# Nine on-chip transposes moved from the DMA crossbar to TensorE, and three weight loads cut into fourteen

## Chip, cores, metric

One core of a Trainium2 chip runs the whole program. The metric is the device time of one execution in microseconds (us). Times are medians of several runs; every run carries the granted TensorE clock of its core. A single profiled execution supplies each trace, and its span is about 2 us shorter than its device time.

## The reference

Attention over four batches of eight heads (sequence 768, head width 64), in which each query keeps only six key chunks of 32, followed by a gated MLP with a spatial mixing matrix.

```python
# q, k, v: (4, 8, 768, 64) float32
ub  = sum(maximum(q * k_min_of_chunk, q * k_max_of_chunk))     # bound of each chunk
sel = the 6 chunks with the highest ub, causal
attn = softmax(where(sel & causal, q @ k.T / 8, -1e9))
x = (attn @ v) as (4, 768, 512)
h = relu(x @ w_in); u, v = halves of h
out = (u * (w_spatial @ layernorm(v) + b)) @ w_out
```

## The kernel before

Two heads are one *pair*; there are 16 pairs, four to a batch. The program is written as steps placed on numbered *beats*, twelve beats to a pair, and the build turns them into one fixed instruction order for each engine. An engine works through its order in turn, so an instruction that waits holds up those behind it; one trace below shows PE standing 11.3 us before a single matmul.

The k of every pair but the first, and the attention output x of every pair but the last, are transposed by DMA through the crossbar:

```python
def k_transpose(self):
    src = self.k.rearrange("p h t d -> p (h t d)")
    if self.i == 0:
        kT = ps_ml.tile([P, 2, NQT // 2, P], F16, tag="mlp", name="kTp")     # PSUM
        ...
        for t in range(NQT):
            nc.tensor.transpose(out[:, t * P:(t + 1) * P], src[:, t * P:(t + 1) * P], identity)
    else:
        kT = sb.tile([P, 2, NQT // 2, P], F16, tag="kT", name="kT")           # SBUF
        nc.sync.dma_start_transpose(out=kT.rearrange("d h m s -> d (h m) s"), in_=src)
# ... k_max, k_min, k_operand read kT on VectorE ...
def x_transpose(self):
    ...
    if self.i < NPAIR - 1:
        nc.sync.dma_start_transpose(out=dst.rearrange("p (t s) -> p t s", s=P),
                                    in_=self.x16.rearrange("p t h d -> p (t h d)"))
    else:
        tr = self.trans_tile()
        for t in range(NQT):
            nc.tensor.transpose(tr[:, t * P:(t + 1) * P], self.x16[:, t, :, :], identity)
        nc.vector.tensor_copy(dst, tr)
```

q, k and v come by GpSimd-issued DMA with a cast to 16 bits, two pairs (384 KB after the cast) at a time, each row in pieces of 64 elements. The three weights come whole, between them:

```python
at(1 * BEATS, load_w_in)        # 1024 KB
at(2 * BEATS, load_w_spatial)   # 1152 KB
at(3 * BEATS, load_w_out)       #  512 KB
# ... the first MLP starts at beat 57; its first matmuls read x of pairs 0 to 3 and w_in
```

The softmax here doesn't subtract the row's maximum and nothing guards it: scores larger than these inputs give would overflow.

## Time and profile before

| | before |
|---|---|
| median of the runs | 250.38 us (247.63 to 255.23) |
| the profiled execution | 258.75 us, span 257.0 us, mean clock 0.934, marked slow |
| first MLP matmul | 81.8 us, then a stall until 89.6 us |

The page of the profile cuts the span into 40 slices of 6.4 us; a digit is the busy share in tenths, PEclk the granted TensorE clock in tenths, DMA the busy share of the core's 16 DMA engines ("the rings" below), GB/s what they moved.

```profile
PE   1256677044986399969997789799999999999994
DVE  4995966061679689999999999977556824338530
PEclk9999795755899979988999999999999999999999
DMA  9999999999999999999519520301250010160006
GB/s 60 114 148 145 113 171 126 95 80 101 156 157 126 137 147 126 98 95 140 78 55 182 165 61 4 64 0 33 106 172 18 18 32 3 34 242 2 0 10 237
```

The DMA row is full up to 122 us, while PE and VectorE (DVE) have a hole in the eighth slice. Here the full row stands over a hole: the engines idle while the loads are still under way. The view by windows puts numbers on it. Its columns are length, busy us (and instruction count) of each engine, granted clock, DMA share and GB/s:

```profile
20.00:40.00 20.00, 12.70 (x168) 9.12 (x168) 14.65 (x55) 13.29 (x26) 7.82 (x9) 0.88 2.01 146
40.00:60.00 20.00, 8.19 (x69) 5.63 (x68) 8.31 (x36) 6.02 (x11) 1.56 (x2) 0.59 2.10 90
60.00:80.00 20.00, 15.77 (x207) 12.11 (x208) 12.10 (x49) 13.46 (x28) 5.23 (x5) 0.85 2.31 150
```

From 40 to 60 us no compute engine is busy half the time, and the rings move 90 GB/s against about 150 on either side. The view of waits over the first 100 us names what stood in front of the engines (total us, times, longest):

```profile
DVE qs_84 L160 <- DMA q<-in_q_dram: 10.4, 1, 10.4
DVE kmm L179 <- DMA kT<-k: 5.0, 2, 2.5
PE wtr L341 <- DMA ws_raw<-in_moe_w_spatial_dram: 4.1, 1, 4.1
PE mlp L375 <- DMA xT<-x_960: 3.1, 1, 3.1
```

The DMA view gives KB of one issue and the median us from issue to landing:

```profile
k<-in_k_dram POOLq DMA_DIRECT2D x7, 384.0 KB, 14.6
ws_raw<-in_moe_w_spatial_dram POOLq DMA_DIRECT2D x1, 1152.0 KB, 42.1
w_out_sb<-in_moe_w_out_dram POOLq DMA_DIRECT2D x1, 512.0 KB, 46.5
kT<-k SPq DMA_TRANSPOSE x15, 6.3
```

In this trace a crossbar transpose lands 2.5 to 2.8 us after its issue once the rings are quiet (from 124 us); in the first 90 us it took 6.2 to 23.1 us.

### The profile page before, as it was taken

What the parts mean: (1) busy time and instruction counts of PE and PEld (TensorE: products, weight loads), DVE (VectorE), ACT (ScalarE), POOL (GpSimd) and SP (SyncE); (2) the same over time, 40 slices, a digit from 0 to 9 for tenths busy, and PEclk for the clock granted to TensorE, in tenths of its full rate; (3) what the DMA queues carried; (4) which work ended last, traced back from release to release, by engine and by line L of the source; (5) the groups of instructions that cost most, each with busy time, mean ns of one, the idle gap of its engine ahead of it and who ended that gap; (6) DMA issues with size and microseconds to landing.
All of it is one profiled execution on the core that took longest, in us unless ns stands there. A gap on an engine that the chain in (4) does not pass through costs nothing.

```text
span 257.0 us, 5354 instructions
## 1 busy us (share of the span) xinstructions
PE 203.3 (79%) x2016; PEld 130.1 (51%) x2016; DVE 180.7 (70%) x608; ACT 165.8 (64%) x323; POOL 69.6 (27%) x94
## 2 busy tenths in 40 slices
PE   1256677044986399969997789799999999999994
PEld 0134455034753256636654456567555666645551
DVE  4995966061679689999999999977556824338530
ACT  3947484041796259935687689666899986657213
POOL 8983342022115623153113103111121122200000
PEclk9999795755899979988999999999999999999999
DMA  9999999999999999999519520301250010160006
GB/s 60 114 148 145 113 171 126 95 80 101 156 157 126 137 147 126 98 95 140 78 55 182 165 61 4 64 0 33 106 172 18 18 32 3 34 242 2 0 10 237
DMA packets 103486, 24.74 MB, mean 96 GB/s; under 512 B 98594, under 2 KB 99874, under 8 KB 103460
## 3 DMA queue, kind: packets, MB, share of 16 engines
q0 software_dynamic: 76000, 12.19, 88.4%
q1 hardware_dynamic: 27460, 12.20, 29.5%
q8 instruction: 16, 0.26, 0.5%
q14 instruction: 10, 0.08, 0.1%
HBM read 24.39 MB, written 6.29 MB: 119 GB/s over the span
## 4 chain that ended last, share of the span: by engine, by line
PE 39%; DMA 30%; DVE 20%; POOL 4%; issue 3%; ACT 3%; SPq 0%; POOLq 0%; ACTq 0%
PE mlp L375 27%; DMA q<-in_q_dram 16%; DMA kT<-k 7%; PE sc L263 5%; PE acc L285 4%; DMA k<-in_k_dram 3%; DMA xT<-x_960 3%; DVE kmm L183 2%; DVE kmm L179 2%; DVE stats L387 2%; PE tr L250 2%; ACT e L268 1%; DVE vn L399 1%; DVE rq L214 1%; DVE gT L415 1%
## 5 line engine op out<-in xcount | busy, mean ns | idle before, releaser
L268 ACT ACTIVATE e<-sc 128x512 f16<-128x512 f32 x192 | 99.4, 555 | 35.5 <-PE sc L263 28.6
L275 POOL TENSOR_SCALAR_AFFINE_SELECT e<-e 128x384 f16<-128x384 f16 x48 | 25.6, 535 | 100.5 <-ACT e L268 100.5
L375 PE MATMUL mlp<-wsT,vn 128*128 128x512 f16 (+1 forms) x192 | 42.9, 330 | 0.0
L285 PEld LDWEIGHTS <-e 128*128 128x128 f16 x672 | 33.5, 101 | 17.1 <-POOL e L275 2.3
L375 PE MATMUL mlp<-w_in_sb,xT 128*128 128x512 f16 x96 | 27.3, 400 | 6.7 <-DMA xT<-x_960 3.1
L415 DVE TENSOR_TENSOR gT<-mlp,uT 128x512 f16<-128x512 f32 (+1 forms) x32 | 17.7, 555 | 12.7 <-PE mlp L375 11.9
L375 PE MATMUL mlp<-xT,w_in_sb 128*128 128x512 f16 (+1 forms) x128 | 25.8, 326 | 0.0
L375 PE MATMUL mlp<-w_out_sb,gT 128*128 128x512 f16 x96 | 25.6, 379 | 0.0
L423 ACT COPY o<-mlp 128x512 f32<-128x512 f32 x24 | 14.2, 592 | 14.7 <-PE mlp L375 13.6
L375 PEld LDWEIGHTS <-vn 128*128 128x128 f16 x192 | 18.3, 99 | 10.0 <-DVE vn L399 0.2
L385 ACT ACTIVATE vraw<-mlp 128x512 f32<-128x512 f32 x24 | 14.5, 605 | 11.4 <-PE mlp L375 11.0
L387 DVE BATCH_NORM_STATS2 stats<-vraw 128x6 f32<-128x512 f32 x24 | 16.5, 688 | 7.3 <-ACT vraw L385 7.2
L179 DVE TENSOR_REDUCE kmm<-kT 128x24 f16<-128x768 f16 x15 | 14.2, 945 | 5.0 <-DMA kT<-k 5.0
L375 PEld LDWEIGHTS <-xT 128*128 128x128 f16 x96 | 9.3, 102 | 15.9 <-DMA xT<-x_960 3.4
L315 POOL DMA_DIRECT2D q<-in_q_dram x9 | 12.0, 1337 | 18.5 <-issue 7.4
L315 POOL DMA_DIRECT2D k<-in_k_dram x9 | 12.1, 1348 | 17.3 <-issue 11.9
L407 ACT ACTIVATE uT<-mlp 128x512 f16<-128x512 f32 (+1 forms) x32 | 15.8, 506 | 1.4 <-PE mlp L375 1.4
L375 PEld LDWEIGHTS <-w_in_sb 128*128 128x128 f16 x128 | 11.8, 98 | 6.7
L183 DVE TENSOR_REDUCE kmm<-kT 128x24 f16<-128x768 f16 x15 | 14.1, 942 | 0.0
L285 PE MATMUL acc<-vt_80,e 128*128 128x65 f16 x210 | 12.3, 199 | 2.3 <-POOL e L275 2.1
L399 DVE TENSOR_SCALAR vn<-vraw,mv,rstd 128x512 f16<-128x512 f32 x24 | 12.1, 555 | 0.7 <-ACT rstd L397 0.7
L375 PEld LDWEIGHTS <-gT 128*128 128x128 f16 x96 | 8.6, 98 | 7.1 <-DVE gT L415 0.4
(243 smaller groups left out, 404.4 us busy)
## 6 DMA issues: line engine op xcount, KB each, us to landing
out_dram<-o SPq DMA_DIRECT2D x24, 256.0 KB, 2.1
k<-in_k_dram POOLq DMA_DIRECT2D x7, 384.0 KB, 14.6
q<-in_q_dram POOLq DMA_DIRECT2D x7, 384.0 KB, 13.1
ws_raw<-in_moe_w_spatial_dram POOLq DMA_DIRECT2D x1, 1152.0 KB, 42.1
w_in_sb<-in_moe_w_in_dram POOLq DMA_DIRECT2D x1, 1024.0 KB, 25.4
vt_82<-in_v_dram POOLq DMA_DIRECT2D x2, 384.0 KB, 14.5
vt_83<-in_v_dram POOLq DMA_DIRECT2D x2, 384.0 KB, 27.8
vt_80<-in_v_dram POOLq DMA_DIRECT2D x2, 384.0 KB, 18.3
```

Source lines behind the costliest of these rows:

```text
L179: nc.vector.tensor_reduce(self.kmm[:, 0, :], self.kT.rearrange("d h m (c ch) -> d (h m c) ch", ch=CHUNK), axis=AX.X, op=Alu.max)
L183: nc.vector.tensor_reduce(self.kmm[:, 1, :], self.kT.rearrange("d h m (c ch) -> d (h m c) ch", ch=CHUNK), axis=AX.X, op=Alu.min, negate=True)
L268: nc.scalar.activation(out=self.e[hi][:, g * 512:g * 512 + width], in_=sc[:, 0:width], func=Act.Exp, scale=scale)
L275: nc.gpsimd.affine_select(out=blk, in_=blk, compare_op=Alu.is_ge, fill=0.0, base=0, channel_multiplier=-1, pattern=[[0, 3], [1, P]])
L285: mm(self.av[:, qi, :], lhsT=self.e[hi][:, c:c + P], rhs=self.v[:, hi, t, 0:D + 1], start=(t == 0), stop=(t == qi))
L315: nc.gpsimd.dma_start(out=t[:, 0:n, :, 0:D], in_=src)
L375: mm(st[group][:, 0:cols], lhsT=lhsT, rhs=rhs, start=(j == 0), stop=(j == n - 1))
L385: nc.scalar.activation(st["vraw"][:, ti, :], h, func=Act.Relu)
L387: nc.vector.bn_stats(stats, st["vraw"][:, ti, :])
L399: nc.vector.tensor_scalar(st["vn"][:, ti, :], in0=st["vraw"][:, ti, :], scalar1=st["mv"][:, ti, 0:1], scalar2=st["rstd"][:, ti, :], op0=Al ...
L407: nc.scalar.activation(st["uT"][:, db, t0:t1], h[:, 0:t1 - t0], func=Act.Relu)
L415: nc.vector.tensor_tensor(st["gT"][:, db, t0:t1], in0=vs[:, 0:t1 - t0], in1=st["uT"][:, db, t0:t1], op=Alu.mult)
```

## The change

The intent is to take transposes off the rings while they are full of loads, and to let k, q and v pass between the pieces of the weights.

```diff
-            if self.i == 0:                      # k_transpose
+            if self.i < 6:
-            if self.i < NPAIR - 1:               # x_transpose
+            if 4 <= self.i < NPAIR - 1:
-    def load_w_in():
-        nc.gpsimd.dma_start(out=w_in_sb, in_=moe_w_in.rearrange("(o p) f -> p o f", p=P))
+    def load_w_in(j):
+        nc.gpsimd.dma_start(out=w_in_sb[:, j], in_=moe_w_in[j * P:(j + 1) * P, :])
 ... load_w_spatial(j) and load_w_out(j) likewise ...
-    at(1 * BEATS, load_w_in)
-    at(2 * BEATS, load_w_spatial)
-    at(3 * BEATS, load_w_out)
+    for j in range(NDO):
+        at(12 + 8 * j, load_w_in, j)
+    for j in range(NQT):
+        at(36 + 4 * j, load_w_spatial, j)
+    for j in range(KO):
+        at(62 + 6 * j, load_w_out, j)
     for so in range(NQT):
-        at(4 * BEATS + 2 * so, prep_w_spatial, so)
+        at(5 * BEATS + 2 * so, prep_w_spatial, so)
```

More of the change, by code (lines that the diff above doesn't have):

```diff
@@ L327, with load_w_spatial, load_w_out @@
     brow_l = cp.tile([P, P], F16)
-    def load_w_in():
-        nc.gpsimd.dma_start(out=w_in_sb, in_=moe_w_in.rearrange("(o p) f -> p o f", p=P))
-    def load_w_spatial():
-        nc.gpsimd.dma_start(out=ws_raw, in_=moe_w_spatial.rearrange("(to ti) s -> ti to s", ti=P))
-    def load_w_out():
-        nc.gpsimd.dma_start(out=w_out_sb, in_=moe_w_out.rearrange("(ko ki) f -> ki ko f", ki=P))
+    def load_w_in(j):
+        nc.gpsimd.dma_start(out=w_in_sb[:, j], in_=moe_w_in[j * P:(j + 1) * P, :])
+    def load_w_spatial(j):
+        nc.gpsimd.dma_start(out=ws_raw[:, j], in_=moe_w_spatial[j * P:(j + 1) * P, :])
+    def load_w_out(j):
+        nc.gpsimd.dma_start(out=w_out_sb[:, j], in_=moe_w_out[j * P:(j + 1) * P, :])
     def prep_w_spatial(so):
```

## The prediction

> **What bounds the kernel now.** The span has two stages. From about 90 us on TensorE bounds it: in the ten-us windows PE is busy 155 of the last 167 us. Before 90 us the DMA rings do. The page's DMA row is 9 in every slice up to 122 us, and over 30 to 60 us PE is busy only 15.1 us of 30, VectorE 15.7, ScalarE 13.0; from 46 to 52 us nothing computes. The chain of waits gives DMA 30%, the largest piece being 41.5 us of one q load (issued 35.6, landed 77.1). The list of waits names VectorE for the third group's q, 10.4 us (to 53.4), PE for the spatial weight, 4.1 us (to 61.2), PE for the last x transpose of batch 0, 3.1 us (to 89.6). Idling also leaves PE at a granted clock of 0.5 in most windows from 40 to 66 us; the Trainium skill ("TensorE: Matmul & The Clock Gate", the HAM clock gate) says the clock halves after an idle window, and this trace agrees.
>
> Loads queue behind each other: the spatial weight (1152 KB) takes 42 us from issue to landing, the output weight 46, k and q loads between them 36 to 45. And crossbar transposes slow everything: one takes 2.5 to 2.8 us when the rings are quiet (from 124 us), 6 to 23 us in the first 90. With up to three in flight (44 to 60 us) the rings move 55 to 107 GB/s, against about 150 at 12 to 28 us with zero to two. From the bytes landed (2.9 MB from 26 to 61 us, 20 us at 150 GB/s, in 35 us with four transposes; 2.3 MB from 77 to 98 us, 15 us, in 21 with two and a half) I estimate 2 to 4 us of ring time per transpose. The skill's "DMA: Bandwidth & Descriptors" (Issuing engines are not separate DMA queues) says why: all queues run on the same 16 engines.
>
> **The change.** It removes nine of 29 transposes, all in the DMA-bound stage: an estimated 18 to 36 us of ring time, nearly all critical. Split weights let k, q and v pass between pieces of 128 to 256 KB. It adds: on PE nine times six transposes, about 0.35 us a set warm, 0.8 cold, 4 us in all; on VectorE four x copies from PSUM (0.56 us each) and 20 operand copies 0.1 us dearer, 4 us; on GpSimd eleven more issues of 0.8 us, mostly in idle time. PE now blocks in order on a late k load, and each k tile holds one of three PSUM buffers for 16 beats; both look affordable.
>
> **Sum.** At 145 GB/s the 6.8 MB needed before the first MLP take about 50 us, so VectorE then sets the pace, 9 to 10 us a pair: the first MLP matmul, now at 81.8 with a stall to 89.6, comes at about 65 us. The PE-bound stage behind it stays 163 to 170 us; the transpose waits near 103 to 113 us (6 us) mostly vanish. Gain about 21 us: **229 us**, range 219 to 239. Faster by over 2%: 0.93; same 0.05; slower 0.02.
>
> **What would show it.** No hole at 46 to 60 us; the q wait under 3 us; loads landing in under 20 us; rings near 150 GB/s up to 60 us, load traffic over by about 100 us instead of 123; first MLP matmul at 60 to 70 us; clock 1.0 from 30 us on; the last 160 us unchanged.
>
> **What would make it wrong.** The rings may be slow for the weights themselves, not the transposes: then only the queueing gain, 5 to 10 us, is left. PE may wait on k or PSUM buffers. Smaller pieces may be slower.

## The result

The kernel after takes **234.78 us** (234.45 to 235.37, four runs); before took 249.42 us beside it (247.63 to 255.23). The ratio is 0.944, interval 0.937 to 0.951. Ratios here are the mean time of one kernel's fast runs over that of the other's fast runs of the same rounds, so they are not quite the ratios of the medians quoted. Executions over 1.5% slower than the fastest of the same kernel are left out of the means. The time lies inside the stated range, and the gain is 14.6 us where 21 was forecast.

The page of the kernel after (slices of 5.8 us):

```profile
PE   0349888788959989898699989999999999999992
DVE  4899999999999999999999999772669235266520
PEclk9999999999999999999799999999999999999999
DMA  8999999999999049925945011014320501420015
GB/s 54 109 146 157 183 165 185 165 161 174 162 157 146 15 51 157 105 62 152 146 144 53 19 37 34 3 34 164 142 26 12 26 12 37 161 109 0 3 76 195
```

The hole is gone, the clock is 1.00 until 110 us, the rings are full only to 76 us, and the VectorE row now is what the DMA row was: full. By windows:

```profile
20.00:40.00 20.00, 17.69 (x255) 13.26 (x253) 19.31 (x76) 16.55 (x34) 12.29 (x17) 1.00 2.06 173
40.00:60.00 20.00, 16.41 (x221) 11.19 (x219) 19.37 (x69) 18.33 (x39) 10.59 (x13) 1.00 1.96 168
60.00:80.00 20.00, 17.30 (x207) 11.38 (x205) 19.47 (x68) 13.17 (x27) 6.37 (x8) 1.00 1.73 125
...
60.00:140.00 80.00, 70.88 (x750) 45.05 (x748) 77.97 (x259) 57.88 (x117) 21.56 (x30) 0.98 1.00 99
```

VectorE is busy 19.3 of 20 us where it was busy 8.3, and 78 of 80 us from 60 to 140 us. The Trainium skill ("TensorE: Matmul & The Clock Gate", the HAM clock gate) says that PE's clock halves after an idle window and is full again after a busy one. These traces agree: the clock was 0.59 on average from 40 to 60 us before, with PE busy 8.2 of 20 us, and 1.00 after, with PE busy 16.4 us. In the waits of the first 100 us, the four lines shown of before have no successor: the longest wait of a compute engine for a DMA is now the very first k, which before had as well (5.6 us).

```profile
PE kTp L171 <- DMA k<-in_k_dram: 5.4, 1, 5.4
```

And the loads land sooner (the kT line is not like for like: the ten transposes left are those of pairs 6 to 15, mostly after the loads):

```profile
k<-in_k_dram POOLq DMA_DIRECT2D x7, 384.0 KB, 11.2
ws_raw<-in_moe_w_spatial_dram POOLq DMA_DIRECT2D x6, 192.0 KB, 12.1
w_out_sb<-in_moe_w_out_dram POOLq DMA_DIRECT2D x4, 128.0 KB, 14.3
kT<-k SPq DMA_TRANSPOSE x10, 4.0
```

The first MLP matmul starts at 61.1 us instead of 81.8. Behind it the span is 233.3 - 61.1 = 172.2 us, against 257.0 - 81.8 = 175.2 before. So 20.7 of the 23.7 us between the two *profiles* came before the first MLP. That is more than the 14.6 us between the *times*, because the profile of before shows a slow execution.

### The profile page after: what moved, and what is told of

The parts are those of the page before. It is cut to its first block, busy times and chain, and to the rows that moved or that the text cites. A ratio compares the mean times of both kernels' runs of the same rounds, so it can differ in the third digit from the quotient of the medians.

```text
span 233.3 us, 5451 instructions
## 1 busy us (share of the span) xinstructions
PE 200.4 (86%) x2070; PEld 128.8 (55%) x2070; DVE 183.0 (78%) x612; ACT 165.8 (71%) x323; POOL 74.6 (32%) x105
## 3 DMA queue, kind: packets, MB, share of 16 engines
q1 hardware_dynamic: 20260, 10.43, 19.6%
## 4 chain that ended last, share of the span: by engine, by line
DVE 44%; PE 41%; ACT 8%; issue 3%; DMA 3%; POOL 0%; ACTq 0%; POOLq 0%; DVEq 0%
PE mlp L375 26%; PE sc L263 6%; ACT e L268 5%; DVE kmm L179 5%; PE acc L285 4%; DVE kmm L183 4%; DVE stats L387 3%; DVE vn L399 3%; DVE km_88 L191 2%; DVE km_89 L191 2%; DVE rq L214 2%; DVE rq L216 2%; DMA k<-in_k_dram 2%; PE tr L250 2%; DVE gT L415 1%
## 5 line engine op out<-in xcount | busy, mean ns | idle before, releaser
L268 ACT ACTIVATE e<-sc 128x512 f16<-128x512 f32 x192 | 99.2, 558 | 23.7 <-PE sc L263 17.6
L285 PEld LDWEIGHTS <-e 128*128 128x128 f16 x672 | 32.3, 98 | 17.4 <-issue 4.5
L415 DVE TENSOR_TENSOR gT<-mlp,uT 128x512 f16<-128x512 f32 (+1 forms) x32 | 17.6, 554 | 12.3 <-PE mlp L375 11.5
L375 PE MATMUL mlp<-w_out_sb,gT 128*128 128x512 f16 x96 | 26.4, 390 | 0.0
L375 PE MATMUL mlp<-w_in_sb,xT 128*128 128x512 f16 x96 | 25.4, 379 | 0.1
L423 ACT COPY o<-mlp 128x512 f32<-128x512 f32 x24 | 14.2, 592 | 15.8 <-PE mlp L375 14.2
L387 DVE BATCH_NORM_STATS2 stats<-vraw 128x6 f32<-128x512 f32 x24 | 16.4, 685 | 4.8 <-ACT vraw L385 4.6
L399 DVE TENSOR_SCALAR vn<-vraw,mv,rstd 128x512 f16<-128x512 f32 x24 | 13.4, 610 | 0.7 <-ACT rstd L397 0.7
L375 PEld LDWEIGHTS <-xT 128*128 128x128 f16 x96 | 8.7, 98 | 7.0 <-issue 0.2
L285 PE MATMUL acc<-vt_80,e 128*128 128x65 f16 x210 | 11.6, 193 | 0.2 <-POOL e L275 0.2
L292 DVE RECIPROCAL rec<-acc 128x6 f32<-128x6 f32 x32 | 5.8, 183 | 7.3 <-PE acc L285 7.1
L285 PE MATMUL acc<-vt_83,e 128*128 128x65 f16 x168 | 9.2, 193 | 2.5 <-DVE x_1200 L293 2.5
## 6 DMA issues: line engine op xcount, KB each, us to landing
k<-in_k_dram POOLq DMA_DIRECT2D x7, 384.0 KB, 11.2
vt_83<-in_v_dram POOLq DMA_DIRECT2D x2, 384.0 KB, 11.5
```

The source lines that it names most:

```text
L268: nc.scalar.activation(out=self.e[hi][:, g * 512:g * 512 + width], in_=sc[:, 0:width], func=Act.Exp, scale=scale)
L285: mm(self.av[:, qi, :], lhsT=self.e[hi][:, c:c + P], rhs=self.v[:, hi, t, 0:D + 1], start=(t == 0), stop=(t == qi))
L375: mm(st[group][:, 0:cols], lhsT=lhsT, rhs=rhs, start=(j == 0), stop=(j == n - 1))
L387: nc.vector.bn_stats(stats, st["vraw"][:, ti, :])
L399: nc.vector.tensor_scalar(st["vn"][:, ti, :], in0=st["vraw"][:, ti, :], scalar1=st["mv"][:, ti, 0:1], scalar2=st["rstd"][:, ti, :], op0=Al ...
L415: nc.vector.tensor_tensor(st["gT"][:, db, t0:t1], in0=vs[:, 0:t1 - t0], in1=st["uT"][:, db, t0:t1], op=Alu.mult)
```

## The experiments

Three theories. **R** (ring time, the prediction's): while loads are queued, each crossbar transpose takes 2 to 4 us of the rings, whoever waits for it. **L** (landing): the rings lose little; what costs is that someone waits for the late landing of a transpose. **Q** (queueing): k, q and v wait behind whole weights. Each ratio is to the kernel before in the same rounds.

### Control: the kernel before again

No edit.

> The kernel before, unchanged, for a profile in the fast state (the one at hand took 258.75 us, 4% over the fastest run). All theories: ratio 1.00, 247 to 250 us. If the slow state stretches the DMA-bound stage, the first MLP matmul comes several us before the 81.8 us of the slow profile and the hole without any engine busy (46 to 52 us) is shorter; if it stretches the PE-bound stage, the first MLP matmul stays at 80 to 83 us.

Measured: 256.8 us median (255.64, 257.95, 261.11, 247.47), the kernel before beside it 250.76 (247.66 to 257.14). The profile again fell into a slow execution (span 253.9 us, clock 0.939). So the same program scatters from 247.5 to 261.1 us. The two slow profiles still say something: the first MLP matmul comes at 78.4 us here and at 81.8 there, 3.4 us apart, and the spans are 3.1 us apart. What differs between these two executions lies in the load-bound stage. The kernel after, which issues three crossbar transposes in the first 70 us where before issued seven, scattered by 0.4%.

### Weights alone

```diff
-            if self.i < 6:                       # from the kernel after: both transposes
+            if self.i == 0:
-            if 4 <= self.i < NPAIR - 1:
+            if self.i < NPAIR - 1:
```

> Only the weights split and spread; all transposes stay on the crossbar. Theory R (ring time: each crossbar transpose takes 2 to 4 us of the rings while loads are queued): little gain, 244 to 249 us, ratio 0.98 to 1.00, rings still full to about 115 us. Theory Q (queueing: k, q, v wait behind whole weights): most of the gain, 236 to 240 us, ratio 0.95 to 0.965.

Measured: 248.7 us, ratio 0.982 (0.968 to 0.997; two of the four runs were slow and are not in it). This is what R expected, though the build blurs the test of Q: the loads do land sooner (the median of the spatial weight's pieces is 16.5 us), but PE then waits 7.5 us in one place for an x transpose, and the rings stay nearly full (one slice of 40 excepted) until after 110 us. The wait depends on the order that this build got: in the traces the first MLP matmul is about the 236th matmul of PE here, against the 501st before and the 550th after (the spatial weight's transposes also stay one pair later, as in the kernel after). So this run does not say what cutting the weights would gain in a better order. What speaks against Q as the main cause is the next run.

### Transposes alone

```diff
-            if self.i == 0:                      # from the kernel before
+            if self.i < 6:
-            if self.i < NPAIR - 1:
+            if 4 <= self.i < NPAIR - 1:
```

> Only the nine transposes moved to PE; the three whole weight loads stay. Theory R: most of the gain, 236 to 240 us, ratio about 0.955, first MLP matmul at 63 to 68 us. Theory Q: little gain, 245 to 249 us, with q of the third group and the spatial weight still waited for 5 us and more.

Measured: **234.89 us** (234.60 to 235.69), ratio 0.938 (0.933 to 0.943). This is the whole gain, somewhat more than R's range, with the weights still loaded in three pieces. First MLP matmul at 64.8 us. Cutting the weights adds nothing once the transposes are gone. It costs nothing either: pieces of 128 to 256 KB do no worse than whole loads of 512 to 1152 KB here. The Trainium skill ("DMA: Bandwidth & Descriptors", Rules for kernel authors) asks for at least 1 MiB per DMA for most bandwidth; with always several loads queued, these runs show no difference.

### Ghost transposes

The kernel after computes as it did, and the nine crossbar transposes are issued as well, into a tile that nothing reads.

```diff
                     nc.tensor.transpose(out[:, ...], src[:, ...], identity)
+                if self.i > 0:
+                    spare = sb.tile([P, 2, NQT // 2, P], F16, tag="spare", name="spare")
+                    nc.sync.dma_start_transpose(out=spare.rearrange("d h m s -> d (h m) s"), in_=src)
 ...
                 nc.vector.tensor_copy(dst, tr)                    # x_transpose
+                if self.i < 4:
+                    spare = sb.tile([P, NQT, P], F16, tag="spare", name="spare")
+                    nc.sync.dma_start_transpose(out=spare, in_=self.x16.rearrange("p t h d -> p (t h d)"))
```

> The kernel after, plus the same nine crossbar transposes issued at the same places into a spare tile that nothing reads: ring load back, no consumer waits for their landing. Theory R: the gain goes again: 242 to 248 us, load traffic over at 95 us or later instead of 76. Theory L (what cost time was the latency that k and x consumers wait for, 6 to 23 us a transpose, not the ring time): within 1.5% of the kernel after, 234 to 238 us.

Measured: 246.46 us, ratio 0.975 (0.963 to 0.987). More than half of the gain is gone (the ratio was 0.944 without the ghosts), as R said; the profile is of a slow execution. But it showed a fault of the experiment. x lives in two buffers, so VectorE had to wait 11.0 us until a ghost had read one. Nobody waited for the ghost's output, but somebody waited for its input, and L could still be right.

### Ghost transposes that nobody can wait for

As above, with more buffers:

```diff
-                self.x16 = sb.tile([P, NQT, 2, D], F16, tag="x16", name="x16")
+                self.x16 = sb.tile([P, NQT, 2, D], F16, tag="x16", name="x16", bufs=6)
-        ... sb.tile([P, 4, NQT, D], F16, tag=name, name=name, bufs=3)
+        ... sb.tile([P, 4, NQT, D], F16, tag=name, name=name, bufs=6 if name == "k" else 3)
```
and `bufs=9` for the spare tiles.

> The ghost kernel with six buffers for k and for x in place of three and two, so that nothing has to wait for a ghost to have read its source (in the ghost kernel VectorE waited 11.0 us for one). The compiled orders of PE, VectorE and ScalarE are those of the kernel after, entry for entry. Theory R (ring time): still 242 to 247 us, because the loads themselves land later. Theory L (the wait for a transpose's landing, whoever waits, is the cost): 235 to 238 us, at most 1.5% over the kernel after.

Measured: **248.79 us** (246.91 to 249.17), ratio 1.009 (0.994 to 1.024), above even R's range. L falls as a full account and R stands. The compiled orders of PE, VectorE and ScalarE equal those of the kernel after entry for entry (on GpSimd one k load sits one mask step earlier), no engine touches a ghost, and 14.0 us come back. No run has the larger buffers without the ghosts; but the ghost kernel above, without them, slowed down too. The DMA view shows the loads landing later; its lines for k and for the ghosts:

```profile
k<-in_k_dram POOLq DMA_DIRECT2D x7, 384.0 KB, 17.4
spare<-k SPq DMA_TRANSPOSE x5, 8.6
spare<-x SPq DMA_TRANSPOSE x4, 10.3
```

The k loads take 17.4 us to land instead of 11.2. The windows where VectorE had been full:

```profile
60.00:80.00 20.00, 13.59 (x133) 8.47 (x132) 13.61 (x45) 8.79 (x17) 7.55 (x11) 0.83 1.84 143
80.00:100.00 20.00, 14.40 (x137) 9.57 (x135) 12.26 (x42) 10.83 (x24) 6.26 (x7) 0.83 2.77 146
```

VectorE did not wait for a load itself in these stretches. The way led through GpSimd, which issues the loads and also applies the causal mask to e; the waits of this run show both links:

```profile
POOL w_out_sb L342 <- DMA vt<-in_v_dram: 7.9, 1, 7.9
PE acc L288 <- POOL e L278: 11.2, 3, 5.6
```

From 60.6 to 68.5 us GpSimd stood before issuing a piece of the output weight, until a v load had landed (at 68.2). The mask behind it in GpSimd's order came late, and PE waited 5.2 us for it. So here the ring time cost because an engine that works in order stood before a late *load*, though nobody read the ghosts.

How much ring time is one transpose? The rings are full up to the landing of the sixth q load in all three kernels below, so its landing (issue plus issue to landing) can be compared:

| kernel | sixth q landed | over the kernel after | per extra DMA |
|---|---|---|---|
| after | 57.1 us | | |
| nine plain copies (below) | 63.5 us | 6.4 us | 0.7 us |
| nine ghosts, free | 77.2 us | 20.1 us | 2.2 us |

In both kernels all nine extra DMAs had been issued by then (the last of the plain copies only just, at 61.8 us, and it landed after, at 68.3). This is an estimate: late landings also delay later issues, so part of the 20.1 us is feedback. A second estimate comes from the pages, which put the packets of the sync engine's queue at 19.6% of the span after, 22.9% with plain copies and 27.6% with free ghosts: the extra packets make 1.0 and 2.5 us for each DMA. Packets of different queues overlap, so this is rough too.

### Plain copies of the same bytes

The ghost kernel with `dma_start` in place of `dma_start_transpose`:

```diff
-    nc.sync.dma_start_transpose(out=spare.rearrange("d h m s -> d (h m) s"), in_=src)
+    nc.sync.dma_start(out=spare.rearrange("d h m s -> d (h m s)"), in_=src)
 ... and the x copy likewise ...
```

> The ghost kernel with its nine unread crossbar transposes replaced by nine plain SBUF to SBUF copies of the same bytes at the same places. If the bytes take the ring time, as slow as the ghost kernel: 243 to 247 us. If it is the transposing (many 256-byte pieces through the crossbar), the copies cost little: 234 to 238 us, load traffic over before 85 us.

Measured: 237.78 us (236.53 to 238.71), ratio 0.948 (0.938 to 0.959). So the bytes cost about 3 us of the end time. The two fast runs of the ghost kernel (242.89 and 245.50), which has the same buffers, lie 9.4 us above the kernel after on average; the transposing costs the rest. The page counts packets on the sync engine's queue: 20,260 in the kernel after, 27,460 before and 21,556 here. That makes (27,460 - 20,260) / 9 = 800 packets for one transpose (in the packed trace 768 of 256 bytes and 32 of 4), and (21,556 - 20,260) / 9 = 144 packets for a copy of the same 196,608 bytes (128 of 1,536 bytes and 16 of 4). The transpose moves the same bytes in five and a half times as many packets. Whether the packets or the crossbar itself sets its price, these runs do not separate.

### Which of the nine: k on PE, x on the crossbar

```diff
-            if 4 <= self.i < NPAIR - 1:          # from the kernel after
+            if self.i < NPAIR - 1:
```

> The kernel after with the four x transposes of batch 0 back on the crossbar (k on PE, weights split). Theory R (ring time, each alike): five of nine gone, so 237 to 242 us; nearer 237 if VectorE and not the rings sets the pace once most are gone. If one of the two kinds carries it all (x because the first MLP waits for its landing), 246 to 249 us.

Measured: **250.56 us** (249.71 to 253.04), ratio 1.003 (0.992 to 1.014). Neither expectation holds: five of nine are gone and nothing is gained. The waits between 40 and 90 us:

```profile
PE mlp L375 <- DMA xT<-x: 16.2, 3, 11.3
DVE rec L292 <- PE acc L285: 10.1, 1, 10.1
```

and the windows:

```profile
50.00:60.00 10.00, 3.81 (x36) 2.87 (x37) 0.20 (x1) 1.47 (x3) 0.00 (x0) 0.50 1.95 142
```

PE stood 11.3 us in front of an MLP matmul that reads the x of pair 1, whose crossbar transpose was issued at 43.2 and landed at 56.1 us. In-order PE held up the attention behind it, and VectorE did 0.2 us of work in ten. It was the second MLP matmul (the expectation of the run with a later MLP, below, calls it the first). In this build the MLP had been placed early in PE's order: its first matmul is about the 317th of PE, against the 550th in the kernel after.

### Which of the nine: x on PE, k on the crossbar

```diff
-            if self.i < 6:                       # from the kernel after
+            if self.i == 0:
```

> The kernel after with the five k transposes back on the crossbar (x on PE, weights split). Theory R: four of nine gone, 239 to 244 us. If the k transposes carry it all (bounds and operands of every pair wait for kT), 246 to 249 us; if the x transposes do, 235 to 237 us.

Measured: 241.89 us (240.27 to 242.47), ratio 0.966 (0.956 to 0.975), inside R's range. First MLP matmul at 65.5 us; VectorE waits 2.7 us for a kT.

With the weights cut in all four, the ratios to the kernel before form a square (in brackets about which matmul of PE the first MLP matmul is):

| | x on crossbar | x on PE |
|---|---|---|
| k on crossbar | 0.982 (236th) | 0.966 (509th) |
| k on PE | 1.003 (317th) | 0.944 (550th) |

The k transposes are worth 7.1 us (241.89 - 234.78) when x is off the crossbar and nothing in the two builds that leave x on it. The parts do not add, so "each alike" was too simple for these builds. But each build also has its own order, and both on the left place the MLP early, before a late x; the square does not separate the transposes from the order.

### A later MLP for the kernel with x on the crossbar

```diff
+        late = 12 if b == 0 else 0               # from "k on PE, x on the crossbar"
-        first, count = (b + 1) * HP * BEATS + 9, HP * BEATS
+        first, count = (b + 1) * HP * BEATS + 9 + late, HP * BEATS - late
```

> The k_w kernel (x on the crossbar; 250.6 us) with the first MLP starting twelve beats (one pair) later and squeezed into the 36 beats left. In k_w PE stood 11.3 us in front of its first MLP matmul, which waited for an x transpose issued 13 us earlier. Theory L: with a pair more between x and its reader the wait is hidden and most of the 16 us come back: 236 to 243 us. Theory R: the ring time is unchanged, 247 to 252 us.

Measured: 242.23 us (239.84 to 244.62), ratio 0.981 (0.960 to 1.001); its profile is of a slow execution. With a pair more between the x transposes and their reader, 8.3 of the 15.8 us lost come back by the medians, and 2.2 of 5.9 points by the ratios, whose interval here is wide. The first MLP matmul is now about the 618th of PE. So part of the loss in the build before was a matter of order, and L has a share: the landing time of a transpose costs when an in-order engine stands in front of it. With this order the five k transposes gone come to about what the four x transposes gone gave (242.23 and 241.89 us). A wait of the same kind is left: PE waits 11.5 us for the spatial weight's pieces.

### Lightening VectorE: three tries for a better kernel

VectorE is the new bound, so three moves off it were tried, each from the kernel after. First, the six copies of the transposed spatial weight:

```diff
-        nc.vector.tensor_copy(wsT[:, so, :], tr)
+        nc.scalar.copy(wsT[:, so, :], tr)
```

> The kernel after with the six copies of the transposed spatial weight moved from VectorE to ScalarE. After the change VectorE is busy 9.7 to 9.8 of every 10 us from 10 to 140 us, and ScalarE 4.7 of 10 from 60 to 70 us. If VectorE is the new bound there, its 3.2 us come off: 231 to 233 us. If PE or ScalarE holds that stage, 234 to 236 us.

Measured: 238.77 us, ratio 0.956 (0.946 to 0.966), slower than either expectation.

Second, the q copies of pairs 6 to 15:

```diff
+            eng = nc.gpsimd if self.i >= 6 else nc.vector
-            nc.vector.tensor_copy(self.qs[:, :, 0, D:2 * D], self.q[:, 0])
-            nc.vector.tensor_copy(self.qs[:, :, 1, 0:D], self.q[:, 1])
+            eng.tensor_copy(self.qs[:, :, 0, D:2 * D], self.q[:, 0])
+            eng.tensor_copy(self.qs[:, :, 1, 0:D], self.q[:, 1])
```

> The kernel after with the two q copies of pairs 6 to 15 moved from VectorE to GpSimd, which is 15 to 30% busy after 70 us. VectorE loses about 0.5 us a pair, 5 us in all, in the stage where it is 97% busy (to 140 us). If VectorE's load bounds that stage, 231 to 233 us; if what matters there is the order in which the in-order engines meet, 234 to 239 us, as moving the weight copies to ScalarE showed (238.8 us).

Measured: 238.99 us, ratio 0.973 (0.954 to 0.992).

Third, the four x copies out of PSUM:

```diff
-                nc.vector.tensor_copy(dst, tr)
+                (nc.scalar.copy if self.i < 4 else nc.vector.tensor_copy)(dst, tr)
```

> The kernel after with the four copies of the transposed x out of PSUM on ScalarE instead of VectorE (the pace of the first 60 us is VectorE's, 9.7 of 10 us busy; ScalarE is at 8 to 9). If VectorE's work alone sets the pace of that stage, the first MLP matmul comes 2 us earlier and the time is 232 to 233 us. If the pace is set by how the in-order engines meet, as the two other moves off VectorE showed, 235 to 240 us.

Measured: 235.04 us (234.88 to 238.09), ratio 0.939 (0.931 to 0.948). The first MLP matmul does come 2.1 us earlier (59.0 us), but the stage behind it is 2.0 us longer (174.2 us).

None beats the kernel after. In the first two, VectorE is busy 71.0 and 74.5 us of the 80 from 60 to 140 us, instead of 78.0, and PE 66.4 and 67.8 instead of 70.9: less to do, and less done. Each of the three edits also changed the compiled order of PE (854 to 1,396 lines of a diff of some 4,100 rows, in which a moved row counts twice). Whether the order is the cause was argued, not shown; no run here holds it fixed.

## Why the prediction was right, and where it was off

- **Rings bound the first 90 us: right.** Taking nine transposes off them filled VectorE from 8.3 to 19.4 of 20 us between 40 and 60 us, and putting them back with nobody waiting for them cost 14.0 us, with the orders of PE, VectorE and ScalarE unchanged.
- **2 to 4 us of ring time per transpose: right at its low end.** 2.2 us by the landing of the sixth q load, against 0.7 us for a plain copy of the same bytes.
- **The step "nine of 29 transposes ... nearly all critical" was too simple.** There were 30 (15 of k, 15 of x). In the build with x left on the crossbar, removing k's five gains nothing, because PE, with the MLP placed early, stands 11.3 us in front of one x; with the MLP later 8.3 us of that come back. What a transpose costs depends on the order around it.
- **The queueing gain of "5 to 10 us" was mis-sized.** It measured 1.8% alone (interval 0.3 to 3.2%) in a build that puts the MLP early, and nothing on top of the transposes (234.89 against 234.78 us).
- **VectorE then sets the pace, 9 to 10 us a pair, first MLP at about 65 us: right.** The x copies out of PSUM start at 34.5, 43.4, 51.9 and 60.5 us, 8.7 us a pair; the first MLP matmul is at 61.1 us. The added costs were about right as well: 0.56 us for an x copy, 0.35 us against 0.25 us for an operand copy, and 0.50 us from the first start to the last end of six x transposes.
- **"The PE-bound stage behind it stays 163 to 170 us": off.** It measured 172.2 us and is not PE-bound until about 140 us: VectorE is busy 78 of the 80 us from 60 to 140. The last 160 us did stay alike: PE is busy 148.8 us of them, 148.3 before. The first MLP came 4 us sooner than forecast and the stage behind it took 2 to 9 us longer, so that the two misses partly cancel; that is luck.
- **The sum: 21 us forecast, 14.6 measured.** The gain between the two profiles is 23.7 us, about as forecast, and the prediction's own two stages (65 and 163 to 170) add up to a span of 228 to 235 us, where 233.3 was measured. The term that was mis-sized is the base. Every number of the first stage was read from an execution of 258.75 us, and the gain was then taken off a median of 250.38. The 9 us between the traced execution and the later median (249.42) were counted as if the change could win them. The two slow profiles of the same program differ by 3.4 us in the first stage and 3.1 us in all, which suggests that the 9 us lie there too; no profile of a fast execution of before exists, so that is not shown.
- **The signs.** No hole; no q wait; loads landing within 15.9 us; 168 to 173 GB/s from 20 to 60 us; first MLP matmul at 61.1 us. The clock was 1.00 to 110 us, then 0.83 for ten us. "Load traffic over by about 100 us" was off in kind: the full stretch ends at 76 us, and the last v load, whose issue waited for PE until 109.9 us, lands at 115.8 us.

## What to carry to other kernels

Here a DMA transpose landed in 2.5 to 2.8 us on quiet rings and was dear beside queued loads, where it delayed the loads by an estimated 2.2 us and also landed late in front of an in-order reader; in that stage six TensorE transposes of about 0.5 us in all were the better tool. To tell bandwidth from latency, issue the suspected transfer again with no reader, and make sure that nobody waits for its source buffer either. Compare the instruction orders of two builds before putting their difference down to the edit. Check the state of the traced execution before taking a gain read from it off a median of other runs.

## What the Trainium skill lacked or had wrong

- "DMA: Bandwidth & Descriptors" (Latency and other measured facts) gives a DMA transpose an effective 261 GB/s, more when contiguous. Beside queued loads, one SBUF to SBUF transpose of 196,608 bytes took an estimated 2.2 us of the rings here, which is 89 GB/s, and a plain copy of the same bytes 0.7 us; this is the delay to other loads, not the time of a transpose on its own. The page does not say what a transpose costs the other transfers.
- The same page (Alternative transpose paths) names TensorE as a way to transpose, but neither it nor another page weighs the two by how full the rings are. Here nine transposes moved to it were worth 6.2% (ratio 0.938 for that part alone).
- The same page (Rules for kernel authors) asks for 1 MiB or more per DMA. Weights in pieces of 128 to 256 KB ran as fast as whole ones (234.78 against 234.89 us) with other loads always queued.
